# Attention and a two-layer MLP on one core: w_in asked behind the first value chunk, fifteen small matmuls in front, and a held Pool copy moved behind an addition

## The chip, the cores and the metric

The kernel runs on one core of a Trainium2 chip. The core has a matrix engine (PE, whose weight loads the profile lists as PEld), a vector engine (DVE), a scalar engine for activations (ACT), a general engine (Pool, also written POOL or GpSimd), a queue engine (SP), and 16 DMA engines that move data between the off-chip memory, HBM, and the on-chip memory, SBUF. PE writes its results to PSUM, an accumulation memory of eight banks; DVE and ACT read them from there. All engines run their own list of instructions in order and wait for each other through semaphores.

The metric is device time in microseconds (us). Three runs of the kernel before took 312.16, 312.55 and 313.92 us; the median is 312.55.

## The reference, cut to what matters

Inputs q, k and v have 8 batches, 8 heads, 576 positions and 64 features. Each batch gets two attentions whose results are added, and the sum goes through two matrix products with a quick GELU between them.

```python
factor = 4
q_d = q.reshape(B, H, Sd, factor, D).mean(axis=3)       # k_d, v_d likewise: 144 positions
out_up = np.repeat(sm_attn(q_d, k_d, v_d), factor, axis=2)
mask = np.abs(pos[:, None] - pos[None, :]) < factor     # local attention, 7 neighbours
scores = np.where(mask, scale * q @ k.T, -1e9)
out_local = softmax(scores) @ v
x = (out_up + out_local).transpose(0, 2, 1, 3).reshape(4608, 512)
h = x @ w_in                                            # 512 x 2048
g = h * sigmoid(1.702 * h)
out = g @ w_out                                         # 2048 x 512
```

## The kernel before, in words

The order of the work is written out by hand: each engine's instructions stand in the order in which the code calls them, and semaphores are put in where one needs the other's result.

The MLP works on nine groups of 512 tokens. In a group, `mm1` computes 16 chunks of 128 hidden features, each from four matmuls of 128x512 over `xT` (the attention's output, transposed, in four tiles of 128 features) and `w_in_bf` (line 813, called through `hps_mm`); ACT applies the activation (line 824). `mm2` then makes four tiles of 128 tokens from 16 matmuls each with `w_out_bf` (line 891). The attention of the next batch is cut into steps that are called at fixed places between these matmuls: `POS_0` lists the places for group 0, `POS` those for the later groups. Place 16 is the first matmul of `mm2`. For batch 1 the steps are: scores of the first four heads, their exponentials, scores and exponentials of the other four, and then one step for each of the four pairs of heads (`avx1`). The last of a pair's work is an addition (line 664) that adds the coarse attention to the local one in `xT`; for the first three pairs Pool does it, for the fourth DVE. The products in front of it are DVE's (line 653), which reads copies that it took out of PSUM (line 642) and ACT's logarithms and exponentials (lines 637 and 648).

Batch 0 has nothing to hide behind. Its attention runs first, and group 0 starts behind it. At the start, DVE sets constants while Pool asks for batch 0's k and q (line 218) and for its values in five chunks (line 259, `load_vb0`). PE begins with `warm(2)`, two float32 matmuls on zeros (line 777), writes the mask into PSUM with `bars0` (line 411) and then computes scores (line 423) as soon as DVE has transposed q and k (line 311). It reduces the value chunks to the coarse values with selection matrices (line 388, `prep_vd_pe`) in the order of the chunks, and needs chunks 3 and 4 last.

Pool asks for the weights behind batch 0's loads. Two iotas (line 116, `iota_band`) come first, then a copy of one element of value chunk 1 into `gate` (line 943): it holds Pool until that chunk has landed. Then come w_in in three pieces (line 281), batch 1's k and q, and w_out's first two pieces (line 290), then batch 1's values in ten pieces (line 249), w_out's last two pieces and batch 2's k and q. Each of Pool's DMAs uses one of eight semaphores in turn and waits for the landing of the DMA eight before it; so w_out's second piece waits for w_in's first one, and the pieces of batch 1's values for those in between.

Batch 2's float32 values are loaded through SP's queue by `load_v(2, gate=...)` (line 238). Its gate is one more copy of a single element on Pool (line 929), out of w_out's last piece: Pool stands until that has landed, then SP's ten loads may go. In the program before it stands on Pool ahead of batch 1's three additions of line 664. On SP's queue the output stores of group 0 and further loads of batch 2 stand behind the ten loads.

In group 0, `hps_mm` splits the matmuls of the last three of the four feature tiles into two halves of 256 tokens for the first nine chunks, and in group 1 for the first eight; the other matmuls are whole.

Of the kernel before, what the change touches and what calls it, by code (L numbers as in the profile page):

```python
# [19 lines left out]
def kernel(  # L20
# [9 lines left out]
    nc = tc.nc  # L30
# [30 lines left out]
    w_out_bf = persist.tile([128, n_ffc, d_model], BF16, name="w_out_bf")  # L61
    xT = [persist.tile([128, B * S], BF16, name=f"xT{i}") for i in range(HP)]
    vbs = [persist.tile([128, 5, H, 65], BF16, name=f"vb{i}") for i in range(2)]
# [11 lines left out]
    PM = [psum.tile([128, 512], FP32, name=f"pm{i}") for i in range(2)]  # L75
# [3 lines left out]
    def pm_tile():  # L79
        turn["m"] += 1  # L80
        return PM[turn["m"] % 2]

    wz = consts.tile([128, 512], BF16, name="wz")
# [16 lines left out]
    gate = consts.tile([1, 1], BF16, name="gate")  # L100
# [13 lines left out]
    def iota_band():  # L114
        for par in range(2):
            nc.gpsimd.iota(dm[halves[par]], pattern=[[-1, 60]], base=-4 * par,
                           channel_multiplier=1, **it)
# [113 lines left out]
    def load_v(b, gate=None, chunks=range(5)):  # L231
        t = ldp.tile([128, 5, H, D], FP32, name="vf", tag="vf")
        vf[b] = t
        if gate is not None:
            gate(t[0:1, 0, 0, 0:1])
        for i in chunks:
            for par in range(2):
                nc.sync.dma_start(
                    out=t[64 * par : 64 * par + 64, i],
                    in_=bass.AP(  # L240
                        tensor=v.tensor,
                        offset=v[b, 0].offset + (114 * i + KSTART[par]) * D,
                        ap=[[D, 64], [S * D, H], [1, D]],
                    ),
                )
# [12 lines left out]
    def load_vb0(i):  # L258
        nc.gpsimd.dma_start(
            out=vbs[0][:, i, :, 0:D],  # L260
            in_=bass.AP(
                tensor=v.tensor, offset=v[0, 0].offset + 114 * i * D,
                ap=[[D, 128], [S * D, H], [1, D]],
            ),
        )
# [23 lines left out]
    def load_w_out(c):  # L289
        nc.gpsimd.dma_start(  # L290
            out=w_out_bf[:, 4 * c : 4 * c + 4, :],
            in_=bass.AP(
                tensor=moe_w_out.tensor, offset=moe_w_out.offset + c * 512 * d_model,
                ap=[[d_model, 128], [128 * d_model, 4], [1, d_model]],
            ),
        )
# [20 lines left out]
    def prep_qk(b, qd):  # L317
        prep_1("k", b, qd)
        prep_1("q", b, qd)
# [48 lines left out]
    def flat(p):  # L368
        return p.rearrange("p x n -> p (x n)")

    def prep_vd_pe(b, pv, kcs=range(3), eng=None, between=None):
        vb, vd = vbs[b], vds[b]

        def heads(x, j):
            if b == 0:
                return x.rearrange("p (hp j) d -> p hp j d", j=2)[:, :, j]
            return x.rearrange("p (m u j) d -> p m u j d", m=2, u=2)[:, :, j]

        for kc, iis in ((0, (0, 1)), (1, (1, 2, 3)), (2, (3, 4))):
            if kc not in kcs:  # L380
                continue
            c0 = 256 * (kc - kcs[0])
            for i in iis:
                if between:
                    between(kc, i)
                n = S - 114 * i if (b, i) == (0, 4) else 128
                for j in range(2):
                    nc.tensor.matmul(
                        pv[64 * j : 64 * j + 64, c0 : c0 + D * HP],
                        lhsT=psel[b][i // 4][0:n, PSEL_AT[i, kc] : PSEL_AT[i, kc] + 64],  # L390
                        rhs=heads(vb[0:n, i, :, 0:D], j),
                        start=(i == iis[0]), stop=(i == iis[-1]),
                        tile_position=(0, 64 * j),
                    )
        cp = eng.tensor_copy if eng else nc.scalar.copy
        cp(
            out=vd[:, kcs[0] : kcs[-1] + 1, :, 0:D],
            in_=pv[:, 0 : 256 * len(kcs)].rearrange(
                "p (k h d) -> p k h d", k=len(kcs), h=HP
            ),  # L400
        )
# [186 lines left out]
    def sub(t, off, *dims):  # L588
        return bass.AP(
            tensor=t.tensor, offset=t.offset + off,  # L590
            ap=[list(t.ap[0])] + [list(d) for d in dims],
        )
# [181 lines left out]
    def warm(n, t=None):  # L774
        t = pm_tile() if t is None else t
        for _ in range(n):
            nc.tensor.matmul(
                sub(t, 0, (256, 2), (1, 256)), lhsT=wzf[:, 0:128],
                rhs=wzf[:, None, :].to_broadcast([128, 2, 256]),
                start=True, stop=True,  # L780
            )

    def attention(b):
        st = {}

        def s_pe(qd):
            P = PB if b == 1 else PA
            st["d", qd], st["s", qd] = scores_mixed(b, qd, P)

        def s_act(qd):  # L790
            if qd == 0:
                nc.scalar.preload_act_table_set("natural_log_exp_and_others")
            if qd:
                exp_down(qd, st["d", qd])
            exp_local(qd, st["s", qd], (1, 0) if qd else (0, 1))
            if not qd:
                exp_down(qd, st["d", qd])
            mask_local(qd)

        def s1():  # L800
            s_pe(1)
            s_act(1)

        first = [lambda: s_pe(0), lambda: s_act(0), s1]
        if b == 1:
            return first + [lambda hp=hp: avx1(b, hp) for hp in range(HP)]
        return first + [lambda: avx(b, (0, 1)), lambda: avx(b, (2, 3))]

    def hps_mm(g, ffc, dmc, acc):
        halved = dmc and (ffc < 9 if g == 0 else g == 1 and ffc < 8)  # L810
        n = TG // 2 if halved else TG
        for c in range(0, TG, n):
            nc.tensor.matmul(  # L813
                acc[:, c : c + n],
                lhsT=w_in_bf[:, dmc, ffc * 128 : (ffc + 1) * 128],
                rhs=xT[dmc][:, g * TG + c : g * TG + c + n],
                start=(dmc == 0), stop=(dmc == n_dmc - 1 and c + n == TG),
            )

    def new_gT():  # L820
        return moe_sb.tile([128, n_ffc, TG], BF16, name="gT", tag="gT")
# [101 lines left out]
    POS_0 = [16, 18, 28, 40, 48, 58, 69]  # L923
# [4 lines left out]
    def after(src, eng):  # L928
        return lambda t: eng.tensor_copy(out=t, in_=src)
# [9 lines left out]
    fill()  # L939
    for i in range(5):  # L940
        load_vb0(i)
    iota_band()
    nc.gpsimd.tensor_copy(out=gate, in_=vbs[0][0:1, 1, 0, 0:1])
    load_w_in(0, 512)
    load_w_in(512, 512)
    load_w_in(1024, 1024)
    for qd in range(NQ):
        load_qk(1, qd)
    load_w_out(0)
    load_w_out(1)  # L950
    warm(2)
    make_up()
    make_psel0()
# [6 lines left out]
        rhs=wzf[:, None, 0:196].to_broadcast([128, 2, 196]),  # L960
        start=False, stop=True, skip_group_check=True,
# [79 lines left out]
    for g in range(n_groups):  # L1041
        b = g + 1
        if g == 0:
            for i in range(5):
                load_vb(1, i)
            load_w_out(2)
            load_w_out(3)
            for qd in range(NQ):
                prep_qk(1, qd)
                reduce_qk(1, qd, "k")  # L1050
                reduce_qk(1, qd, "q")
                load_qk(2, qd)
            make_psel1()
            nc.gpsimd.memset(v4[32:64], 0.0)
            load_v(2, gate=after(w_out_bf[0:1, 12, 0:1], nc.gpsimd))
        elif b < B:
            load_v4(b)
            prep_qk(b, 0)
            pool_qk(b, 0)
            if 2 < b < B - 1:  # L1060
                for qd in range(NQ):
                    load_qk(b + 1, qd)
            prep_v(b, nc.gpsimd)
            if b + 1 < B:
                load_v(b + 1)
            prep_qk(b, 1)
            if b == 2:
                reduce_qk(b, 1, "k")
                reduce_qk(b, 1, "q")
            else:  # L1070
                pool_qk(b, 1)
            prep_v4(b, nc.gpsimd, (0,))
            if b == 2:
                for qd in range(NQ):
                    load_qk(b + 1, qd)
            prep_v4(b, nc.gpsimd, (1, 2))
        steps = {}
        if b < B:
            for n, f in zip(POS if g else POS_0, attention(b)):
                steps.setdefault(n, []).append(f)  # L1080
            if g == 0:
                steps.setdefault(VDP_0, []).append(lambda: prep_vd_pe(1, flat(PB[2])))
        gT = new_gT() if g else gT0
        mm1(g, gT, steps)
        mm2(g, gT, {n - 16: f for n, f in steps.items() if n >= 16})
# [30 lines left out]
```

## Time and profile before

One execution was profiled.

| what | value |
|---|---|
| time of the profiled execution | 312.91 us |
| its span, first to last instruction | 311.1 us |
| median of three runs | 312.55 us |
| PE busy | 302.7 us, 97% of the span |
| ACT, DVE, Pool busy | 203.3, 149.6, 147.6 us |
| granted PE clock | 1.000 |
| DMA traffic | 39.94 MB in 64042 packets |
| PE instruction blocks fetched | 32, 0.52 MB |

How to read it: rows of the timeline give the start and the time taken in us, then the engine, the line, the operation, output and input tile, the shape, the count of instructions merged, and in square brackets the idle time ahead of it and what ended that. The row of a chain gives its start, its length and what took that time; "issue" is time in which the profile shows no wait. Rows of DMA issues give the engine whose queue asked, the count, the size of one in KB (counted in the written type) and the time from the request to the landing. Matmuls overlap: the end of one is modelled, so groups can overlap by some tenths of a us.

### The profile page before, as it was taken

The page shows a single profiled execution, that of the slowest core. Times are in us where ns is not written, and L with a number is a line of the kernel's source. Part 1 is how long each engine was busy: PE and PEld are TensorE (multiplying, and loading weights), DVE is VectorE, ACT ScalarE, POOL GpSimd, SP SyncE. Part 2 cuts the span into 40 slices and gives each one's busy share as a digit, 9 for nine tenths or more (in the row PEclk, how much of TensorE's full clock was granted, in tenths as well). Part 3 has the DMA queues.
Part 4 walks back from the last instruction along what each step waited for, and adds up shares of the span by engine and source line. Part 5 has one row for each costly group of instructions (what it writes and reads, how often), then busy time and mean ns, then how long its engine had stood idle before and what let it go on. Part 6 is the DMA issues. An engine that isn't in the chain of part 4 may idle for free.

```text
span 311.1 us, 9625 instructions
## 1 busy us (share of the span) xinstructions
PE 302.7 (97%) x4175; PEld 157.1 (51%) x4175; DVE 149.6 (48%) x303; ACT 203.3 (65%) x325; POOL 147.6 (47%) x169
## 2 busy tenths in 40 slices
PE   7799999999999999999999999999999999999995
PEld 3477444664544464455545554555455544444444
DVE  5982957762594159505970499028902760000000
ACT  4748755877858786668866895689558857216611
POOL 8542394288029933795369634983396110000000
PEclk9999999999999999999999999999999999999999
DMA  6999999889937942695169715991520110010011
GB/s 107 135 200 211 184 111 209 184 262 174 202 135 168 207 123 77 171 228 139 70 164 202 177 38 170 190 211 46 155 71 34 39 67 2 34 67 36 0 67 67
DMA packets 64042, 39.94 MB, mean 128 GB/s; under 512 B 44544, under 2 KB 54912, under 8 KB 64000
## 3 DMA queue, kind: packets, MB, share of 16 engines
q0 software_dynamic: 18784, 14.95, 34.4%
q1 hardware_dynamic: 45072, 24.32, 28.0%
q8 instruction: 32, 0.52, 0.7%
q14 instruction: 10, 0.08, 0.1%
q10 hardware_dynamic: 144, 0.07, 0.1%
HBM read 44.83 MB, written 9.44 MB: 174 GB/s over the span
## 4 chain that ended last, share of the span: by engine, by line
PE 83%; DMA 11%; ACT 2%; DVE 2%; POOL 1%; issue 1%; POOLq 0%; DVEq 0%; ACTq 0%
PE pm L891 36%; PE pm L813 22%; PE pa L813 14%; DMA w_out_bf<-in_moe_w_out_dram 6%; PE pa L439 3%; DMA vb<-in_v_dram 2%; DMA w_in_bf<-in_moe_w_in_dram 2%; PE pa L700 2%; PE pa L678 2%; PE pa L466 2%; PE pm L908 1%; DVE xT L653 1%; PE pa L891 1%; ACT l L637 1%; ACT l L648 1%
## 5 line engine op out<-in xcount | busy, mean ns | idle before, releaser
L891 PE MATMUL pm<-w_out_bf,gT 128*128 128x512 bf16 x528 | 119.4, 379 | 0.5 <-DMA w_out_bf<-in_moe_w_out_dram 0.5
L813 PEld LDWEIGHTS <-w_in_bf 128*128 128x128 bf16 x627 | 60.6, 98 | 61.7 <-issue 0.3
L813 PE MATMUL pm<-xT,w_in_bf 128*128 128x512 bf16 (+1 forms) x364 | 88.5, 372 | 0.0
L891 PEld LDWEIGHTS <-gT 128*128 128x128 bf16 x560 | 52.7, 98 | 63.0 <-issue 1.1
L824 ACT ACTIVATE gT<-pm 128x512 bf16<-128x512 f32 x88 | 52.8, 604 | 38.8 <-PE pm L813 38.8
L813 PE MATMUL pa<-xT,w_in_bf 128*128 128x512 bf16 (+1 forms) x263 | 59.1, 347 | 0.0
L511 DVE TENSOR_TENSOR es<-es,mask 128x600 bf16<-128x600 bf16 x28 | 18.0, 683 | 82.4 <-ACT es L477 82.4
L876 ACT ACTIVATE osb<-pm 128x512 f32<-128x512 f32 (+2 forms) x35 | 20.3, 581 | 30.5 <-PE pm L891 28.0
L824 ACT ACTIVATE gT<-pa 128x512 bf16<-128x512 f32 x56 | 31.8, 611 | 6.8 <-PE pa L813 6.8
L770 POOL TENSOR_TENSOR xT<-xT,od 128x576 bf16<-128x576 bf16 x12 | 15.8, 1320 | 41.5 <-DVE xT L754 41.4
L754 DVE TENSOR_TENSOR xT<-n,l 128x285 bf16<-128x285 f32 (+1 forms) x96 | 28.1, 364 | 0.0
L342 POOL TENSOR_TENSOR pq<-kT 128x576 f32<-128x576 bf16 x11 | 12.8, 1161 | 30.4 <-DVE kT L311 26.5
L878 DVE TENSOR_SCALAR osb<-pm 128x128 f32<-128x128 f32 x1 | 0.3, 293 | 53.8 <-ACT osb L876 53.8
L359 POOL TENSOR_TENSOR pq<-v 112x512 f32<-112x512 f32 x18 | 23.7, 1318 | 0.8 <-DMA v<-in_v_dram 0.8
L311 DVE STREAM_TRANSPOSE kT<-kb 128x576 f32<-128x576 f32 x16 | 19.9, 1243 | 6.8 <-DMA kb<-in_k_dram 6.8
L311 DVE STREAM_TRANSPOSE qT<-qb 128x576 f32<-128x576 f32 x16 | 19.8, 1237 | 0.3 <-DMA qb<-in_q_dram 0.2
L503 ACT ACTIVATE ed<-pa 128x864 bf16<-128x864 f32 x16 | 14.3, 894 | 7.9 <-PE pa L466 7.9
L477 ACT ACTIVATE es<-pa 128x600 bf16<-128x600 f32 x28 | 17.2, 670 | 0.1
L749 ACT ACTIVATE l<-l 128x1440 f32<-128x1440 f32 x12 | 16.8, 1404 | 0.4
L744 DVE COPY n<-pa 128x492 f32<-128x492 f32 x24 | 15.0, 665 | 2.3 <-ACT l L743 1.7
L743 ACT ACTIVATE l<-pa 128x492 f32<-128x492 f32 x24 | 12.6, 578 | 4.2 <-PE pa L700 3.6
L439 PE MATMUL pa<-qT,kT 32*64 32x60 bf16 x1120 | 15.3, 195 | 0.0
(133 smaller groups left out, 354.2 us busy)
## 6 DMA issues: line engine op xcount, KB each, us to landing
out_dram<-osb SPq DMA_DIRECT2D x34, 256.0 KB, 2.0
vf<-in_v_dram SPq DMA_DIRECT2D x60, 128.0 KB, 4.9
v<-in_v_dram SPq DMA_DIRECT2D x72, 96.0 KB, 2.8
kb<-in_k_dram POOLq DMA_DIRECT2D x16, 288.0 KB, 5.8
qb<-in_q_dram POOLq DMA_DIRECT2D x16, 288.0 KB, 8.6
w_out_bf<-in_moe_w_out_dram POOLq DMA_DIRECT2D x4, 512.0 KB, 18.4
w_in_bf<-in_moe_w_in_dram POOLq DMA_DIRECT2D x2, 512.0 KB, 7.9
w_in_bf<-in_moe_w_in_dram POOLq DMA_DIRECT2D x1, 1024.0 KB, 13.1
```

The source lines that it names most:

```text
L311: nc.vector.transpose(out=t32.rearrange("p (i c) -> p c i", c=18), in_=store[b, qd].bitcast(FP32).rearrange("p (c d) -> p c d", c=18),)
L359: eng.tensor_tensor(out=t1[0:112], in0=x[:, :, 0:2, :], in1=x[:, :, 2:4, :], op=ALU.add)
L439: nc.tensor.matmul(P[1 + r // 2][64 * par : 64 * par + 64, r % 2, 60 * i : 60 * i + 60], lhsT=kT[b, qd][rows, k0 : k0 + 64, a], rhs=qT[b, ...
L477: nc.scalar.activation(out=es[2 * qd + u][:, :, 0:300], in_=sp[u][:, :, 0:300], func=AF.Exp, scale=inv_sqrt_d,)
L511: nc.vector.tensor_tensor(out=ev, in0=ev, in1=mask, op=ALU.mult)
L749: nc.scalar.activation(out=l, in_=l, func=AF.Exp, scale=-1.0)
L754: nc.vector.tensor_tensor(out=out, in0=sub(n, *part), in1=sub(l, *part), op=ALU.mult)
L770: eng.tensor_tensor(out=xs, in0=xs, in1=sub(od[:, u, :], 0, (1, SD), (0, 4)), op=ALU.add)
L813: nc.tensor.matmul(acc[:, c : c + n], lhsT=w_in_bf[:, dmc, ffc * 128 : (ffc + 1) * 128], rhs=xT[dmc][:, g * TG + c : g * TG + c + n], star ...
L824: nc.scalar.activation(out=gT[:, ffc, :], in_=acc, func=AF.Silu, scale=GELU_SCALE)
L876: eng.activation(out=osb, in_=ap, func=AF.Copy, scale=1.0 / GELU_SCALE)
L891: nc.tensor.matmul(ops[t], lhsT=gT[:, ffc, t * 128 : (t + 1) * 128], rhs=w_out_bf[:, ffc, :], start=(ffc == 0), stop=(ffc == n_ffc - 1),)
```

## The change

There are four edits.

1. The copy that holds w_in reads value chunk 0 instead of chunk 1, and it stands ahead of the two iotas instead of behind them. Pool's order is now: five value chunks, copy, two iotas, w_in.
2. A new function `small` issues 15 matmuls of 32 rows, 64 columns of weights and 60 moving columns on the zero tile, in front of `warm(2)`. They go in turn to four places in two PSUM tiles that nothing has used yet.
3. In group 0 only the first four chunks have halved matmuls, not the first nine: five chunks with three matmuls each become whole, 15 matmuls and 15 weight loads fewer. PE's list has as many instructions as before.
4. `load_v(2)` with its gate copy moves into batch 1's step list, behind the first pair's step. On Pool the copy now stands behind the first addition of line 664 and ahead of the second.

```diff
+    def small(n):
+        for i in range(n):
+            r, c = i % 2, i // 2 % 2
+            rows = slice(32 * r, 32 * r + 32)
+            nc.tensor.matmul(
+                PM[r][64 * c : 64 * c + 64, 0:60],
+                lhsT=wz[rows, 0:64], rhs=wz[rows, 0:60],
+                start=True, stop=True, tile_position=(32 * r, 64 * c),
+            )
...
-        halved = dmc and (ffc < 9 if g == 0 else g == 1 and ffc < 8)
+        halved = dmc and (ffc < 4 if g == 0 else g == 1 and ffc < 8)
...
+    nc.gpsimd.tensor_copy(out=gate, in_=vbs[0][0:1, 0, 0, 0:1])
     iota_band()
-    nc.gpsimd.tensor_copy(out=gate, in_=vbs[0][0:1, 1, 0, 0:1])
     load_w_in(0, 512)
...
+    small(15)
     warm(2)
...
             nc.gpsimd.memset(v4[32:64], 0.0)
-            load_v(2, gate=after(w_out_bf[0:1, 12, 0:1], nc.gpsimd))
...
                 steps.setdefault(VDP_0, []).append(lambda: prep_vd_pe(1, flat(PB[2])))
+                steps[POS_0[3]].append(
+                    lambda: load_v(2, gate=after(w_out_bf[0:1, 12, 0:1], nc.gpsimd))
+                )
```

## The prediction

> **What bounds the kernel now.** I read the busy times first, then the busy times by stage, then the chain that ended last in order of time, then each engine's rows around its links.
>
> ```profile
> span 311.1 us, 9625 instructions
> PE 302.7 (97%) x4175; PEld 157.1 (51%) x4175; DVE 149.6 (48%) x303; ACT 203.3 (65%) x325; POOL 147.6 (47%) x169
> q8 instruction: 32, 0.52, 0.7%
> ```
>
> PE is busy for 302.7 of 311.1 us, so only 8.4 us of PE idle time exist. The table by stage says where it lies; its columns are the stage in us, its length, the busy time (and instructions) of PE, weight loads, DVE, ACT and Pool, and then PE's granted clock, the DMA share and GB/s.
>
> ```profile
> 14.00:15.60 1.60, 1.59 (x31) 1.09 (x28) 1.48 (x3) 1.60 (x3) 1.60 (x4) 1.00 0.68 48
> 15.60:20.60 5.00, 4.57 (x121) 3.58 (x117) 3.93 (x8) 2.28 (x6) 2.83 (x5) 1.00 1.18 194
> 20.60:36.00 15.40, 15.40 (x147) 9.85 (x140) 9.66 (x13) 11.09 (x22) 4.84 (x7) 1.00 1.15 209
> 36.00:44.00 8.00, 7.44 (x240) 4.12 (x218) 6.12 (x15) 5.82 (x8) 5.21 (x8) 1.00 2.29 107
> 44.00:58.00 14.00, 13.67 (x195) 6.87 (x192) 9.08 (x24) 7.56 (x14) 7.76 (x8) 1.00 1.09 196
> 58.00:307.00 249.00, 249.00 (x3366) 126.08 (x3364) 108.58 (x212) 167.23 (x261) 116.23 (x119) 1.00 0.48 121
> ```
>
> From 58 us to 307 us PE never stops: nothing that the change does there can shorten the kernel. Between 20.6 and 58 us PE misses 0.56 us (8.00 - 7.44) and 0.33 us (14.00 - 13.67), together 0.89 us: the ceiling of any gain behind batch 0's attention. The rest lies before 20.6 us, in batch 0's attention, which loads and DVE set. The chain shows what holds the 0.56 us:
>
> ```profile
> 5.42 7.57 DMA vb<-in_v_dram
> ...
> 13.27 7.05 DMA w_in_bf<-in_moe_w_in_dram
> ...
> 20.61 18.57 DMA w_out_bf<-in_moe_w_out_dram
> ...
> 39.23 1.02 PE pm L891 x4
> ```
>
> Value chunk 1 lands at 12.99, the gate copy lets Pool ask for w_in at 13.27, w_in's first piece lets Pool ask for w_out's second piece at 20.61, and PE, whose work in front of it ends 0.48 us too soon, waits until that lands at 39.18.
>
> **The change, part by part.** First the gate. Pool's rows, and the issue-to-landing rows of the value chunks 1 and 4 of batch 0 (issued at 5.42 and 8.02) and of batch 1's last value piece:
>
> ```profile
> 4.48 4.45 POOL L259 DMA_DIRECT2D vb<-in_v_dram  x5
> 8.90 0.48 POOL L116 IOTA dm<- 64x60 f32 x2
> 13.04 0.18 POOL L943 COPY gate<-vb 1x1 bf16<-1x1 bf16 x1 [3.66 <-DMA vb<-in_v_dram]
> 39.47 2.03 POOL L249 DMA_DIRECT2D vb<-in_v_dram  x3 [2.52 <-DMA w_out_bf<-in_moe_w_out_dram]
> 51.54 0.43 POOL L929 CAST vf<-w_out_bf 1x1 f32<-1x1 bf16 x1 [3.71 <-DMA w_out_bf<-in_moe_w_out_dram]
> 51.94 1.20 POOL L664 TENSOR_TENSOR xT<-xT,od 128x576 bf16<-128x576 bf16 x1
> 53.68 1.21 POOL L664 TENSOR_TENSOR xT<-xT,od 128x576 bf16<-128x576 bf16 x1 [0.54 <-DVE xT L653]
> ```
>
> ```profile
> vb<-in_v_dram POOLq DMA_DIRECT2D x1, 128.0 KB, 7.8
> vb<-in_v_dram POOLq DMA_DIRECT2D x1, 64.0 KB, 3.4
> ```
>
> Chunk 1 landed at 12.99, chunk 4 at 8.02 + 7.8 = 15.82: three chunks in 2.83 us, 0.94 each, so chunk 0 landed near 12.05 (estimated from these rows). The new gate copy runs at 12.10, ends at 12.28; the two iotas that now stand behind it take 0.48; w_in is asked at about 12.82 instead of 13.27, 0.45 us earlier. The table has the room for it: between 14.0 and 15.6 us the DMA moves 48 GB/s, after that 194, a hole of 1.6 x (1 - 48/194) = 1.2 us. From 15.6 to 36 us the stream is full, so an earlier start should move all behind it by the same 0.45: batch 1's k and q, w_out and batch 1's values. Bounds: 0 (the value chunks' tail holds w_in back as now) to 1.2 us (the hole vanishes). I take 0.45, which comes from the events themselves. The iotas' consumer, the mask, is made by DVE only behind batch 0's normalisation; moving them costs nothing more.
>
> What that is worth on PE:
>
> ```profile
> 36.40 0.51 PE L439 MATMUL pa<-qT,kT 32*64 32x60 bf16 x40
> 39.23 1.02 PE L891 MATMUL pm<-w_out_bf,gT 128*128 128x512 bf16 x4 [0.48 <-DMA w_out_bf<-in_moe_w_out_dram]
> 44.32 0.30 PE L388 MATMUL pa<-vb,psel 128*64 128x256 bf16 x2 [0.18 <-DVE es L511]
> 53.29 1.24 PE L891 MATMUL pm<-w_out_bf,gT 128*128 128x512 bf16 x5
> 54.68 0.25 PE L603 MATMUL pa<-ed,vd 48*64 48x144 bf16 x2
> ```
>
> w_out's second piece lands at 38.73 instead of 39.18; PE restarts at 38.78 and gains 0.45 of the 0.48. At 44.32 PE waits 0.18. The row names DVE, but the two products read batch 1's last value chunk, whose last piece, issued third in the group at 39.47, so at about 40.8, landed 3.4 later, at 44.2. That stream moves 0.45 forward as PE does: the 0.18 stays. Sum of the first part: -0.45 (0 to -0.66).
>
> Second, Pool's held copy. Before, it waits at 51.54 for w_out's last piece, and behind it stand batch 1's three additions. DVE at that time:
>
> ```profile
> 48.38 0.96 DVE L653 TENSOR_TENSOR xT<-n,l 128x285 bf16<-128x285 f32 x4
> 49.45 0.99 DVE L642 COPY n<-pa 128x300 f32<-128x300 f32 x2
> 51.48 2.12 DVE L653 TENSOR_TENSOR xT<-n,l 128x285 bf16<-128x285 f32 x4
> 53.70 0.99 DVE L642 COPY n<-pa 128x300 f32<-128x300 f32 x2
> ```
>
> The four products at 51.48 take 2.12 us, those at 48.38 only 0.96: the difference, 1.16, is the length of Pool's addition at 51.94 (1.20), which ran beside them. The addition's operand was ready at 49.34. Moved ahead of the copy it runs from about 49.4 to 50.6, beside DVE's copies out of PSUM, which do not suffer: 0.99 at 53.70 beside Pool's addition at 53.68, 0.99 at 49.45 without one. So DVE gains up to 1.16 us, the copy at 53.70 comes earlier, so does ACT's logarithm that waits for it, and PE, which had finished at 54.53 (53.29 + 1.24) and restarted at 54.68, loses its 0.15 us of waiting. More is not there, since PE has no other hole up to 307 us. The copy itself still waits for the same landing (now 0.45 earlier), so the ten value loads of batch 2 on SP's queue, and the output stores and batch 2's further loads behind them, go out no later; the second addition, now behind the copy, is ready after it. If the copy's 0.43 us fell on DVE's products instead, 0.7 of the 1.16 would still remain. Part two: -0.15 (0 to -0.15).
>
> Third, 15 small products (with 15 weight loads) ahead of the warm-up, and five chunks of batch 0 whose three later products are no longer halved: 15 products and weight loads fewer there.
>
> ```profile
> 4.77 0.41 PE L411 MATMUL pa<-off,id 128*128 128x120 bf16 x2
> 8.35 0.23 PE L423 MATMUL pa<-qT,kT 32*128 32x120 bf16 x2 [1.35 <-DVE qT L311]
> 23.08 1.47 PE L813 MATMUL pa<-xT,w_in_bf 128*128 128x256 bf16 x12
> 29.62 6.25 PE L813 MATMUL pm<-xT,w_in_bf 128*128 128x512 bf16 x28
> ```
>
> The nearest shape is the 32-row, 60-column product: 40 in 0.51, 0.013 each, 0.2 us for 15; the upper bound from two 120-column products in 0.41 right after the start is 0.2 each, 3.1 us. They delay the warm-up and the bars behind it. PE then idles 1.35 us until DVE's q transpose, so 0.2 costs nothing, the upper bound would cost 1.7. I take 0.2, by shape, so 0 on the path. Halves cost 2 x 1.47/12 = 0.24, wholes 6.25/28 = 0.22: a gain of 15 x 0.02 = 0.3 at most, but the groups' ends are modelled, and the shorter group carries its tail over fewer products. Twice 256 columns are 512 columns; I take 0.
>
> The sum is -0.45 - 0.15 = -0.60 on the profiled execution, 312.91 to 312.31. That execution lies 0.36 above the median of the three runs, 312.55; on the median: 311.95. Half a per cent, 1.56 us, is about what a measurement of this kernel can tell from no change.
>
> **Rivals.**
>
> *An instruction block meets the last value chunks (slower).* The 15 pairs shift what PE fetches. The page has 32 blocks for 8350 PE instructions, one per 261. This is one block's traffic, in 13.9 to 16 us:
>
> ```profile
> q8 instruction: 1, 0.02, 4.1%
> ```
>
> 4.1% of 16 engines over 2.1 us is 1.38 us on one DMA engine. Thirty instructions earlier it would be asked for ahead of 14 us, while value chunks 3 and 4 still move. PE's two products on chunk 4 follow its landing at once:
>
> ```profile
> 15.86 0.30 PE L388 MATMUL pm<-vb,psel 120*64 120x256 bf16 x2
> ```
>
> A landing later by x delays batch 0's attention, and with it PE's unbroken run from 20.6 us on, by x. All that can absorb it are the waits of 0.48, 0.18 and 0.15, together 0.81: it decides above x = 0.81, and at x = 1.38 the sum is +0.57, 313.1. For it: the landing at 15.82 has no slack. Against: the chunk's rows are spread over 16 engines and mostly moved by 14.0 (48 GB/s from there). The Trainium skill, "Runtime: NRT & Kernel Launch", section "Instruction fetch mechanics", calls the cost of crossing a 16 KiB block mostly hidden; by that rule x is 0 and 311.95 stands. PE's unbroken stage to 307 us agrees, while no run here shows a block inside these chunks. The skill's "DMA: Bandwidth & Descriptors", section on queues, rings and completion order, says that an engine turns between its queues packet by packet, which would let a whole block stand in front, x up to 1.38.
>
> *The earlier request gains nothing.* The stream is bound by the value chunks and full from 15.6 us, and w_out lands at 39.18 as before. Then only 0.15 is left: 312.4. For it: w_out's second piece shares its stage with batch 1's value pieces (36 to 44 us, DMA share 2.29), which could set its landing; against: the hole of 1.2 us.
>
> *More than counted.* The hole closes and the 0.18 at 44.32 goes too, and chunk 4 lands earlier: -0.66 - 0.15 - 0.2 = -1.0, 311.5.
>
> **How the numbers follow.** Forecast 0.45, no gain from the request 0.14, more 0.11, the block (or small products above the 1.35 us) 0.30. The block alone ends within half a per cent even at its full price; beyond +1.56 it comes only with the small products' upper bound on top (1.38 + 1.7), a third of this case: 0.10, and 0.01 for what is unseen make slower by over 0.5% 0.11. Faster by over 0.5% needs 1.56 where 0.89 is the ceiling behind 20.6 us, so the rest from batch 0's attention: 0.07. The remaining 0.82 is within. The range takes the "more" case and a low run, 311.1, and the block case at its full price with as much above it, 313.5. The forecast's own range is 311.5 to 312.4.
>
> **What the changed profile would show.** The gate copy near 12.1 and w_in asked near 12.8; w_out's second piece landing near 38.7 and no wait above 0.1 us at PE's ninth product of the second layer; Pool's first addition near 49 us and the second head's four products back at about 1 us; PE's wait before the third head's products gone; the score products of batch 0 still starting at 8.35. Wrong if batch 0's chunk 4 lands after 16.4, if the first scores slip beyond 8.5, or if w_out's second piece lands at 39.2 again.

## The result, and the profile after

The changed kernel takes 311.79 us (median of 22 runs, 311.41 to 312.23), the kernel before 312.58 us on the same chips (22 runs, 311.98 to 314.39). The ratio is 0.9971 with a 95% interval of 0.9961 to 0.998. The change is a gain of 0.8 us, 0.3%: certain, because so many runs stand behind it, and inside the half per cent that the prediction had called no change. The forecast was 311.95. Between the two profiled executions the gain is 1.2 us: the time went from 312.91 to 311.70, the span from 311.1 to 309.9. 0.3 of that is the profile of before lying above its median.

The head of the page of the changed kernel:

```profile
span 309.9 us, 9625 instructions
PE 303.5 (98%) x4175; PEld 156.4 (50%) x4175; DVE 148.1 (48%) x303; ACT 203.6 (66%) x325; POOL 147.8 (48%) x169
q8 instruction: 32, 0.52, 0.7%
```

PE's idle time fell from 8.4 to 6.4 us, a part of it only because the small products fill the start; the counts of instructions and of instruction blocks are the same. The table by stage of the changed kernel (stage, length, busy times and counts of PE, weight loads, DVE, ACT and Pool, PE's granted clock, DMA share, GB/s) says where:

```profile
14.00:15.60 1.60, 1.59 (x30) 1.07 (x27) 1.48 (x3) 1.60 (x3) 1.60 (x3) 1.00 1.26 148
15.60:20.60 5.00, 4.62 (x123) 3.55 (x119) 3.99 (x9) 2.35 (x6) 2.65 (x5) 1.00 1.23 208
20.60:36.00 15.40, 15.40 (x129) 8.42 (x125) 11.27 (x15) 11.09 (x22) 4.77 (x7) 1.00 1.18 206
36.00:44.00 8.00, 7.93 (x233) 4.50 (x214) 4.75 (x14) 6.15 (x9) 6.11 (x10) 1.00 1.71 118
44.00:58.00 14.00, 14.00 (x197) 7.28 (x196) 9.11 (x29) 9.59 (x16) 6.02 (x5) 1.00 1.04 197
58.00:306.00 248.00, 248.00 (x3359) 125.45 (x3357) 106.72 (x207) 165.03 (x259) 116.73 (x118) 1.00 0.48 120
```

The hole of the load stream between 14.0 and 15.6 us has filled from 48 to 148 GB/s, and PE's missing time from 36 to 58 us has shrunk from 0.56 + 0.33 to 0.07 us. From there to 306 us PE is busy without a break, as it was before. PE's rows of the changed kernel, to be held against the five of the prediction:

```profile
36.33 0.51 PE L439 MATMUL pa<-qT,kT 32*64 32x60 bf16 x40
36.78 2.76 PE L901 MATMUL pm<-w_out_bf,gT 128*128 128x512 bf16 x12
42.58 0.97 PE L388 MATMUL pa<-vb,psel 128*64 128x256 bf16 x14
52.21 1.24 PE L901 MATMUL pm<-w_out_bf,gT 128*128 128x512 bf16 x5
```

Line 901 is line 891 of before. The first twelve products of the second layer are now one row, and so are the fourteen selection products: the waits of 0.48 and 0.18 us, which stood inside these rows and cut them, have gone. The score products start 0.07 us earlier than before (36.40), the five products of line 901 by 1.08 us (53.29): 1.0 us of the gain arises between these two rows. The rest comes at the wait behind them; the three products of the second layer that follow there start at 54.17 instead of 55.48, 1.31 us earlier, of which 1.2 are left at the end. The gain is larger than the waits that the rows show (0.48 + 0.18 up to there, 0.15 behind it, 0.81 in all), because the end of a matmul is modelled: products of 512 columns start 0.216 us apart in this trace and are drawn 0.38 long, so a row hides about 0.16 us of a wait behind its last product. From start to start the three waits were worth 0.64, 0.37 and 0.24.

Pool's rows of the changed kernel show why the waits went (line 952 is the copy into `gate`, line 939 the held copy):

```profile
4.49 4.46 POOL L259 DMA_DIRECT2D vb<-in_v_dram  x5
11.86 0.18 POOL L952 COPY gate<-vb 1x1 bf16<-1x1 bf16 x1 [2.91 <-DMA vb<-in_v_dram]
11.99 0.41 POOL L116 IOTA dm<- 64x60 f32 x2
12.35 2.27 POOL L281 DMA_DIRECT2D w_in_bf<-in_moe_w_in_dram  x3
18.60 0.75 POOL L290 DMA_DIRECT2D w_out_bf<-in_moe_w_out_dram  x1 [1.10 <-DMA w_in_bf<-in_moe_w_in_dram]
48.42 1.21 POOL L664 TENSOR_TENSOR xT<-xT,od 128x576 bf16<-128x576 bf16 x1 [2.20 <-DVE xT L653]
49.88 0.17 POOL L939 CAST vf<-w_out_bf 1x1 f32<-1x1 bf16 x1 [0.25 <-DMA w_out_bf<-in_moe_w_out_dram]
51.45 1.21 POOL L664 TENSOR_TENSOR xT<-xT,od 128x576 bf16<-128x576 bf16 x1 [1.40 <-DVE xT L653]
```

w_in is asked at 12.35 instead of 13.27, 0.92 us earlier; its first piece lets Pool ask for w_out's second piece at 18.60 instead of 20.61, 2.0 us earlier. That piece landed at 37.53 (before 39.18), and the last piece of batch 1's values at 43.10 (before 44.19); both now come before PE needs them.

The 2.0 us are more than the 0.92 of the request. A load ends in 16 parts in this trace. Of w_in's first piece, 15 had landed at 18.80 before and the sixteenth at 20.32, 1.52 us later; now they end at 18.13 and 18.32. What differs beside the request is the first of the 32 PE instruction blocks in the trace, which moved from 14.53 to 13.93 us and took 1.4 us in both. The experiments come back to it.

DVE's rows of the changed kernel:

```profile
47.31 0.96 DVE L653 TENSOR_TENSOR xT<-n,l 128x285 bf16<-128x285 f32 x4
50.41 0.96 DVE L653 TENSOR_TENSOR xT<-n,l 128x285 bf16<-128x285 f32 x4
51.47 1.00 DVE L642 COPY n<-pa 128x300 f32<-128x300 f32 x2
```

Pool's addition at 48.42 runs ahead of the products at 50.41, which are back at 0.96 us from 2.12. The second addition, at 51.45, lies beside the copies out of PSUM at 51.47, which take 1.00 as they do alone.

The start, PE's first rows in the changed kernel:

```profile
1.19 0.43 PE L787 MATMUL pm<-wz 32*64 32x60 bf16 x15 [1.19 <-DVE wz L126]
1.55 3.78 PE L777 MATMUL pm<-wz 128*128 128x512 f32 x4
8.37 0.23 PE L423 MATMUL pa<-qT,kT 32*128 32x120 bf16 x2 [0.20 <-DVE qT L311]
```

The fifteen small products delay the warm-up by 0.36 us, and the scores start at 8.37 (before 8.35), behind an idle time of 0.20 instead of 1.35.

### The profile page after: what moved, and what is told of

Its sections match the earlier page's. It is cut to its first block, busy times and chain, and to the rows that moved or that the text cites. A ratio compares the mean times of both kernels' runs of the same rounds, so it can differ in the third digit from the quotient of the medians.

```text
span 309.9 us, 9625 instructions
## 1 busy us (share of the span) xinstructions
PE 303.5 (98%) x4175; PEld 156.4 (50%) x4175; DVE 148.1 (48%) x303; ACT 203.6 (66%) x325; POOL 147.8 (48%) x169
## 4 chain that ended last, share of the span: by engine, by line
PE 94%; DVE 2%; DMA 2%; ACT 1%; issue 0%; POOL 0%; DVEq 0%; ACTq 0%; POOLq 0%
PE pm L901 37%; PE pm L823 25%; PE pa L823 16%; PE pa L439 3%; PE pa L901 2%; PE pa L700 2%; PE pa L678 2%; PE pa L466 2%; DMA qb<-in_q_dram 2%; PE pm L918 1%; DVE qT L311 1%; PE pa L575 1%; PE pa L615 1%; PE pa L603 0%; PE pm L388 0%; PE pa L520 0%
## 5 line engine op out<-in xcount | busy, mean ns | idle before, releaser
L823 PEld LDWEIGHTS <-w_in_bf 128*128 128x128 bf16 x612 | 59.2, 98 | 63.1 <-issue 0.3
```

The source lines that it names most:

```text
L823: nc.tensor.matmul(acc[:, c : c + n], lhsT=w_in_bf[:, dmc, ffc * 128 : (ffc + 1) * 128], rhs=xT[dmc][:, g * TG + c : g * TG + c + n], star ...
```

## The experiments

Each edit alone, each pair of edits, and then variants of the two edits that turned out to matter. Kernels that were measured on one chip in turn share their runs of the kernel before, so equal numbers in the third column are the same runs. "w_in" is the time at which Pool asks for it, "block" the start of the first PE instruction block in the trace, "last part" how long the sixteenth part of w_in's first piece landed behind the fifteenth, "w_out" the landing of its second piece; these four are read from the one profiled execution of each kernel.

| kernel | median, us | before, us | ratio (95% interval) | w_in | block | last part | w_out |
|---|---|---|---|---|---|---|---|
| before | | 312.58 | | 13.27 | 14.53 | 1.52 | 39.18 |
| changed | 311.79 | 312.58 | 0.9971 (0.9961 to 0.998) | 12.35 | 13.93 | 0.19 | 37.53 |
| gate_only | 312.46 | 312.61 | 1.0003 (0.9987 to 1.002) | 12.15 | 15.54 | 1.33 | 38.43 |
| small_only | 312.56 | 312.61 | 1.0004 (0.9994 to 1.0014) | 12.80 | 14.33 | 0.31 | 38.13 |
| move_only | 312.72 | 312.61 | 1.001 (0.9993 to 1.0027) | 12.79 | 15.01 | 1.70 | 39.30 |
| no_move | 311.76 | 312.61 | 0.998 (0.9971 to 0.9988) | 12.12 | 13.91 | 0.11 | 37.81 |
| no_gate_edit | 312.77 | 312.63 | 0.9994 (0.9979 to 1.0009) | 13.12 | 14.49 | 0.17 | 38.48 |
| no_small | 312.72 | 312.63 | 1.0003 (0.9983 to 1.0023) | 12.07 | 17.10 | 0.01 | 37.51 |
| small_27 | 311.87 | 312.63 | 0.9978 (0.9966 to 0.999) | 12.25 | 14.08 | 0.81 | 37.27 |
| unheld | 312.22 | 312.63 | 0.9988 (0.9975 to 1.0002) | 9.34 | 16.06 | 0.96 | 37.20 |
| long_warm | 311.72 | 312.44 | 0.9971 (0.9954 to 0.9988) | 12.35 | 14.59 | 1.21 | 37.82 |
| late_gate | 313.90 | 312.44 | 1.0043 (1.0027 to 1.0059) | 14.15 | 14.18 | 0.08 | 39.37 |
| small_15_halves | 313.57 | 312.44 | 1.0037 (1.0019 to 1.0054) | 11.89 | 14.04 | 1.11 | 37.23 |
| small_2 | 311.86 | 312.80 | 0.9975 (0.9961 to 0.9988) | 12.16 | 14.48 | 0.86 | 37.69 |

**Each edit alone.** gate_only is the kernel before with edit 1, small_only with edits 2 and 3, move_only with edit 4.

```diff
# gate_only, against before
-    iota_band()
-    nc.gpsimd.tensor_copy(out=gate, in_=vbs[0][0:1, 1, 0, 0:1])
+    nc.gpsimd.tensor_copy(out=gate, in_=vbs[0][0:1, 0, 0, 0:1])
+    iota_band()
```

> The first edit alone: w_in behind chunk 0 and two iotas. My theory (the earlier request moves the whole stream): w_in asked near 12.4 instead of 13.27, w_out's second piece landing at 38.3 or before, the waits at 39.23 and 44.32 gone, 0.7 to 0.9 us off the span, ratio about 0.9975; the products of the second head still take 2.1 us. Rival (the instruction block, not the request, set w_in's first landing): the block stays near 14.5, w_in's first piece still lands 6 to 7 us behind its request with w_out's second piece at 38.9 to 39.2, at most 0.3 us gained.

```diff
# small_only, against before
-        halved = dmc and (ffc < 9 if g == 0 else g == 1 and ffc < 8)
+        halved = dmc and (ffc < 4 if g == 0 else g == 1 and ffc < 8)
...
+    small(15)
     warm(2)
```

> The 15 small products and the 15 halves less, alone. My theory: nothing on the path, span within 0.1 us of before, the wait at 39.23 still 0.4 to 0.5. Rival (the block's place matters): the block comes near 13.9, w_in's first piece lands near 18.8 instead of 20.3 though it is asked at 13.27, w_out's second piece lands near 38.5 and 0.4 to 0.7 us are gained.

```diff
# move_only, against before
             nc.gpsimd.memset(v4[32:64], 0.0)
-            load_v(2, gate=after(w_out_bf[0:1, 12, 0:1], nc.gpsimd))
...
+                steps[POS_0[3]].append(
+                    lambda: load_v(2, gate=after(w_out_bf[0:1, 12, 0:1], nc.gpsimd))
+                )
```

> Pool's held copy behind the first addition, alone. My theory: the second head's four products take 0.96 instead of 2.12, the wait before the third head (0.15) goes, 0.15 to 0.3 us off the span, waits at 39.23 and 44.32 unchanged. Rival (the addition collides with DVE's copies instead): the copies at 49.4 grow beyond 1.2 us and nothing is gained.

None of the three differs from before: the gains that were expected of gate_only and move_only did not come, and small_only's time is the one expected, though in its profile the wait for w_out is gone. In gate_only w_in is asked 1.1 us earlier, and the wait for w_out goes; but the block comes at 15.54, in the middle of w_in's first piece, w_out's second piece is only 0.75 us earlier, and batch 1's last value piece becomes the wait. In move_only Pool's first addition lies where the prediction wanted it, and the two waits that the load stream sets stay. PE's waiting rows behind 20 us, first of gate_only, then of move_only:

```profile
43.99 0.30 PE L388 MATMUL pa<-vb,psel 128*64 128x256 bf16 x2 [0.59 <-DMA vb<-in_v_dram]
```

```profile
39.35 1.02 PE L901 MATMUL pm<-w_out_bf,gT 128*128 128x512 bf16 x4 [0.43 <-DMA w_out_bf<-in_moe_w_out_dram]
44.49 0.30 PE L388 MATMUL pa<-vb,psel 128*64 128x256 bf16 x2 [0.24 <-DVE es L511]
```

The profiled execution of small_only (311.83 us) is the fastest of its twelve. It waits for no load there, but its products on batch 1's values take 1.35 us, where the changed kernel's row has 0.97: PE stands for 0.13 us ahead of the third of them (at 42.78, with "issue" as releaser). The median, 0.7 us above, suggests that most of its executions lose more; no profile shows where.

```profile
42.35 1.35 PE L388 MATMUL pa<-vb,psel 128*64 128x256 bf16 x14
```

**Each edit left out.** no_move has all but edit 4, no_gate_edit all but edit 1, no_small all but edits 2 and 3; each is the changed kernel with the diff above taken back.

> The changed kernel with the held copy back in its old place: gate and small products only. My theory: 0.15 to 0.3 us slower than the changed kernel, 0.8 to 1.0 us faster than before, with the second head's products back at 2.1 us. Rival (the gains do not add, the copy's move is hidden once the stream is early): same span as the changed kernel within 0.1 us.

> The changed kernel with the gate edit undone: small products and the moved copy only, w_in asked near 13. Theory after the first runs (both the early request and the block's new place are needed, since either one alone leaves w_out's second piece or batch 1's last value piece landing at the edge of PE's need): the block near 14, w_in's first piece without a straggler, but about 312.3 to 312.6, as the small products alone gave. Rival (the small products and the move carry the gain, the single run of the products was unlucky): 311.8 to 312.0.

> The changed kernel without the small products, with the nine halved chunks back: gate and moved copy only. Theory (both needed): the block at 14.5 to 15.6 inside w_in's first piece, whose last part lands 1.3 us or more behind the others, batch 1's last value piece at 43.8 or later, 312.2 to 312.5. Rival (the gate and the move together do it, the products are idle): 311.7 to 311.9.

no_move is as fast as the changed kernel: the moved copy is worth nothing beside the other two. Pool's and DVE's rows of no_move show what became of the clash:

```profile
49.70 0.17 POOL L939 CAST vf<-w_out_bf 1x1 f32<-1x1 bf16 x1 [3.26 <-DMA w_out_bf<-in_moe_w_out_dram]
49.85 1.20 POOL L664 TENSOR_TENSOR xT<-xT,od 128x576 bf16<-128x576 bf16 x1
```

```profile
50.28 0.94 DVE L653 TENSOR_TENSOR od<-n,l 128x144 f32<-128x144 f32 x1 [0.81 <-ACT l L648]
51.15 0.95 DVE L653 TENSOR_TENSOR xT<-n,l 128x285 bf16<-128x285 f32 x4
```

With the stream early, w_out's last piece lands before 49.7, so the addition starts 1.5 us behind the products at 47.41 that it needs (they end at 48.37), not 2.6 as before (49.34 to 51.94). The addition still slows a product of DVE, the one at 50.28 (0.94 instead of 0.31), but no PE wait follows.

no_gate_edit keeps a PE wait for the values, and its time is that of before. So edit 1 is needed.

```profile
44.67 0.30 PE L388 MATMUL pa<-vb,psel 128*64 128x256 bf16 x2 [1.11 <-DMA vb<-in_v_dram]
```

no_small has the earliest request of the three and w_out's piece at 37.51, and its time is that of before all the same. PE's rows of no_small:

```profile
18.56 0.27 PE L575 MATMUL pa<-id,y 128*128 128x117 bf16 x2
19.56 0.21 PE L575 MATMUL pa<-id,y 128*128 128x114 bf16 x1 [0.73 <-issue]
```

PE stands for 0.73 us inside a run of ready products, with no engine or load that it waits for. The first instruction block began at 17.10 there, 3 us later than in the changed kernel and later than the 14.5 to 15.6 that were expected. Its twelve executions run from 311.53 to 315.0 us, so the loss is not in every one. So the small products, which the prediction took for harmless, are needed as well; the question is for what.

**What the small products are for.** Four variants of the changed kernel, all with edits 1 and 4. In small_27 all halves of group 0 are gone and 27 small products lead: PE's list has the same length. In long_warm and small_2 the nine halved chunks of before are kept; a third float32 warm-up, or two small products, make PE's list longer by two products. small_15_halves keeps the nine halved chunks behind 15 small products, so that it is longer by 15.

```diff
# small_27, against the changed kernel
-        halved = dmc and (ffc < 4 if g == 0 else g == 1 and ffc < 8)
+        halved = dmc and g == 1 and ffc < 8
...
-    small(15)
+    small(27)
```

> The changed kernel with 27 small products and no halved chunk in group 0, so the block moves another 24 instructions forward at the same number of instructions. If it only has to be out of w_in's first piece: block near 13.4 to 13.8, chunk 4 still landing near 15.8, the same time as the changed kernel, 311.6 to 312.0. If a block inside the value chunks delays them (the slower rival of the prediction): chunk 4 lands after 16.2 and the time is 0.4 to 1.2 us above the changed kernel. First scores still near 8.4; if 27 products (0.8 us by the 15 that took 0.36) reach past DVE's transpose they start near 8.6.

```diff
# long_warm, against the changed kernel
-        halved = dmc and (ffc < 4 if g == 0 else g == 1 and ffc < 8)
+        halved = dmc and (ffc < 9 if g == 0 else g == 1 and ffc < 8)
...
-    small(15)
-    warm(2)
+    warm(3)
```

> The changed kernel without the small products and with nine halved chunks, but with a third float32 warm-up product: PE is busy longer at the start by 1.7 us at most, with one instruction more, not thirty. Theory (the number of instructions counts, since it sets when the first block is asked for): the block stays behind w_in's request, at 15 to 17, PE runs dry for some tenths between 18 and 20 or w_in's first piece has a straggler above 0.4 us, 312.2 to 312.9. Rival (the extra early work on PE counts): block near 13.9 or no such wait, 311.6 to 311.9.

```diff
# small_2, against the changed kernel (halves as in long_warm)
-    small(15)
+    small(2)
     warm(2)
```

> The gate edit and the move with nine halved chunks, and two small products ahead of two warm-ups: PE's list is longer by two instructions, as with the third warm-up that gave 311.72, but PE's start is no longer busy. If the place of the instructions decides: about 311.7, first scores at 8.4 behind an idle time of about 1.4, the first instruction block before 15, no 0.7 us hole around 18 to 20 us. If the busy start (or the later first scores) decides: 312.5 to 312.9, as without any small product, the block behind 16 us and PE dry by about 0.7 us near 19.6.

```diff
# small_15_halves, against the changed kernel
-        halved = dmc and (ffc < 4 if g == 0 else g == 1 and ffc < 8)
+        halved = dmc and (ffc < 9 if g == 0 else g == 1 and ffc < 8)
```

> The changed kernel with nine halved chunks, so PE has 30 instructions more than before and every later block comes 30 instructions earlier. If only the first block matters: 311.6 to 312.0, the same as the changed kernel. Rival (the fewer halves keep later blocks in good places): a new wait without a releaser on PE behind 60 us and 312.2 or more.

long_warm was meant to tell whether the count of early instructions matters; it came out as fast as the changed kernel (311.72), and the theory that the fifteen are needed fell with it. But it is longer than no_small by two products and two weight loads, so it left open whether its busy start or these four entries of PE's list did it. small_2 tells: it has the same four entries and an idle time of 0.67 us ahead of the scores, and it takes 311.86 where no_small takes 312.72. The two ran on different chips and their intervals just overlap (0.9961 to 0.9988, 0.9983 to 1.0023); the difference of the ratios, 0.28%, is clear of zero all the same (about 0.1 to 0.5%, an estimate from all their runs), and long_warm and small_27 stand on small_2's side. Four entries are enough; 15 or 27 products bring nothing more. The same stretch of PE's rows in small_2, without a stop:

```profile
18.47 0.32 PE L575 MATMUL pa<-id,y 128*128 128x117 bf16 x3
18.63 0.27 PE L575 MATMUL pa<-up,y 128*128 128x167 bf16 x2
```

small_15_halves shows the same thing further down. With 30 entries more in front of batch 1's scores, its PE rows are

```profile
40.02 0.26 PE L439 MATMUL pa<-qT,kT 32*64 32x60 bf16 x7
41.72 0.18 PE L439 MATMUL pa<-qT,kT 32*64 32x60 bf16 x1 [1.44 <-issue]
```

a stop of 1.44 us with no releaser, and not behind 60 us, where a wait had been expected. To see what these stops have in common, PE's records, products and weight loads together, were counted from the start of the trace. The table gives, for each stop, the entry at which PE stopped, the instruction block that landed last before it went on, and the time between the two (unheld and late_gate follow further down).

| kernel | stop, us | entry | block began, ended | PE went on | behind the block's end |
|---|---|---|---|---|---|
| no_small | 0.73 | 448 | 17.10, 18.10 | 19.56 | 1.46 |
| unheld | 0.73 | 448 | 16.06, 17.04 | 18.26 | 1.22 |
| small_15_halves | 1.44 | 1213 | 38.86, 40.42 | 41.72 | 1.30 |
| late_gate | 0.52 | 1211 | 40.85, 42.60 | 44.29 | 1.69 |
| small_only | 0.13 | 1215 | 39.32, 40.93 | 42.78 | 1.85 |

The traces of small_15_halves and late_gate lack some records of products: late_gate's holds 8307 products and weight loads, where the complete ones of the same length hold 8350. (A missing record shows as a gap of 0.16 us with "issue" ahead of a 512-column product, in these two and in long_warm; that is no stop.) late_gate stops at the same product as small_only, the third on batch 1's values, and small_only's trace is complete; so the entries 1211, 1213 and 1215 are one place, near 1216. Five stops, in four different lines of the code, thus stand at two places of the list. The first place follows the first block of the trace, the second follows the fourth: three blocks for about 768 entries, 256 each.

Each stop ends 1.2 to 1.9 us behind the end of a block. The reading is that PE stops because the next block isn't there. The trace names no releaser, but in none of the fourteen traces does PE pass either place less than 1.2 us behind the end of its block. The delay is not a fixed one: gate_only passes the first place without a stop 1.39 us behind its block (18.74 and 17.35), move_only 1.45. The changed kernel has more room, 2.15 us at the first place (17.46 and 15.31) and 1.97 at the second (42.61 and 40.64), and so has small_2 at the first, 2.5.

In small_15_halves the second place falls among the dense score products and is reached at 40.28, before its block has ended; in the changed kernel it falls 2.3 us later, behind eight products of the second layer. small_15_halves takes 1.8 us more than the changed kernel (313.57 - 311.79), and the stop is 1.44 of that. A second cost lies behind its last product: its trace shows a 33rd block, begun at 313.11 where the span has ended at 311.3, and in five of its twelve executions the time exceeds the span by 1.9 to 2.7 us, in all runs of the other variants by 1.7 to 1.9. Against this edit 3 helps: it takes back the entries that edit 2 puts in front.

Why the block at 14 us is late in some kernels can be seen from the 260th entry, about the last one that no prompt block precedes: in the kernels where the block is prompt, it begins 0.05 to 1.2 us behind that entry. The entry is a yardstick for this stretch alone, since the third block of each trace begins 3.7 to 5.1 us ahead of the entry 512 further on. The time from w_in's request to the 260th entry is 0.77 us in the kernel before, 0.98 in the changed one, 1.69 in long_warm and 1.70 in small_2, all prompt; 1.78 in gate_only, where the block begins 1.6 us behind the entry; 2.03 in no_small and 3.9 in unheld, where it begins 3.0 and 2.8 us behind it. So the order of the two requests separates the kernels: a block that is asked for more than about 1.7 us after w_in comes late, as if it stood among w_in's rows. Edit 1 moves w_in ahead; without small products the 260th entry is the first selection product on batch 0's values (line 388), which starts at 14.10 in no_small; with two small products that entry lies ahead of these (13.86), with fifteen among the scores (13.33). That fits gate_only, where edit 1 brings the block late and gains nothing. With edits 2 and 3 and the late request the block is prompt (14.33 in small_only, 14.49 in no_gate_edit), and what is left is the late stream: no_gate_edit's wait of 1.11 us for the values. The limit of 1.7 us is read from one profiled execution of each kernel.

**When to ask for w_in.** unheld is the changed kernel without the copy that holds w_in. late_gate holds it for value chunk 2 with the iotas behind the copy, and has edit 4 and the nine halved chunks, no small products.

```diff
# unheld, against the changed kernel
-    nc.gpsimd.tensor_copy(out=gate, in_=vbs[0][0:1, 0, 0, 0:1])
     iota_band()
...
# late_gate, against the changed kernel without edits 2 and 3
-    nc.gpsimd.tensor_copy(out=gate, in_=vbs[0][0:1, 0, 0, 0:1])
+    nc.gpsimd.tensor_copy(out=gate, in_=vbs[0][0:1, 2, 0, 0:1])
```

> The changed kernel without the copy that holds w_in: w_in is asked right behind the two iotas near 9.4. If the requests are served in order: value chunks land as before (chunk 4 near 15.8), w_out's second piece earlier by up to 1 us, but no wait of PE is left to remove, so 311.6 to 312.0. If w_in's rows mix with the value chunks': chunk 4 lands 0.5 us or more later, batch 0's attention slips by as much, 312.3 to 313.5.

> Gate on value chunk 2 with the two iotas behind it, no small products, nine halved chunks: w_in asked near 14.4, about when PE asks for its first block. Theory (what counts for the block is whether it goes ahead of w_in's rows): the block at 14.4 to 14.8, w_in's first piece with a straggler below 0.5 us, PE never dry, but w_out's second piece not before 39 and batch 1's last value piece behind 44: 312.5 to 313.2. Rival (the block is late by itself): block behind 15 again.

Asking at 9.34 instead of 12.35 doesn't bring w_in's first piece earlier (18.50 against 18.32), probably because of the value chunks in front, the last of which landed at 15.59. The block, though, came at 16.06, and PE stood for 0.73 us at 18.26, so the 311.6 to 312.0 that were expected became 312.22:

```profile
18.26 0.21 PE L533 MATMUL pa<-vd,ed 48*128 48x65 bf16 x2 [0.73 <-issue]
```

late_gate has no small products, so its nearest neighbour is no_small, with chunk 0 in place of chunk 2: 313.90 against 312.72. Its first block is prompt (14.18) and the last part only 0.08 late, but w_in is asked 2.1 us later; w_out's second piece landed at 39.37, and PE waited for it, for the values and, by the reading above, for a block, where a PE that never runs dry had been expected:

```profile
39.41 1.02 PE L901 MATMUL pm<-w_out_bf,gT 128*128 128x512 bf16 x4 [0.69 <-DMA w_out_bf<-in_moe_w_out_dram]
44.29 0.53 PE L388 MATMUL pa<-vb,psel 128*64 128x256 bf16 x6 [0.52 <-issue]
45.30 0.41 PE L388 MATMUL pa<-vb,psel 128*64 128x256 bf16 x4 [0.48 <-DMA vb<-in_v_dram]
```

Of the places tried, chunk 0 gives the lowest time: without a holding copy the block comes late, behind chunk 2 the loads do. unheld is not clearly slower, though, as its interval (0.9975 to 1.0002) overlaps that of the changed kernel.

## Why the prediction was right, step by step

*The bound.* Right: PE's three waits between 38 and 55 us were all that could be gained behind batch 0's attention, and PE is unbroken from there on. The ceiling of 0.89 us was too low, since each of the shown waits hides 0.09 to 0.19 us of its length; from start to start it was 1.2 us.

*The gate.* The mechanism was right and its size too small. The term was 0.45 us and the request moved by 0.92 (by 0.83 in the mean of the profiles: 11.89 to 12.35 in the eight kernels where chunk 0 holds it, 12.79 to 13.27 in the four with chunk 1): chunk 0 landed at 11.80, not at 12.05, because the chunks do not land at even distances, and the copy and the iotas took 0.49 from 11.86 on where 0.72 had been counted. For w_out's second piece the forecast was 38.73, the landing 37.53: a part of that goes with the sixteenth part of w_in's first piece, which the prediction had no term for.

*The wait of 0.18 us was to stay.* Wrong. The prediction moved batch 1's values by the same 0.45 as PE; they moved by 1.09 and PE at that place by 0.7. This is the "more than counted" rival, of which the mechanism (both waits gone) came true, while chunk 4 of batch 0 landed as before (15.77 against 15.82). It had a chance of 0.11 and a time of 311.5; the median lies between it and the forecast.

*The held copy.* Right in each row (addition at 48.42, products back at 0.96, PE's wait gone) and wrong in its worth: no_move reaches the same time without it. The term of 0.15 was counted beside the gate's, and the earlier landing of w_out's last piece had taken it already.

*The small products.* They took 0.43 us where 0.2 had been counted, and nothing of it lies on the path: right, as far as their own time goes. The step that failed is that the edit was costed by the time of its matmuls alone. It left out that every entry of PE's list moves the places at which a block has to be there. no_small and small_2 show that two small products are worth 0.86 us beside the earlier request, and small_15_halves that, behind 15 small products, the halves taken back are worth 1.8. So that the forecast came so close is in part luck, since two errors met: too little for the gate with the others' help, and nothing for the others. The gate by itself, which the sum gave 0.45 us, gained nothing (gate_only, no_small).

*The instruction block.* The slower rival had the right object and the wrong victim. The block did move 0.6 us forward and took 1.38 us, exactly the price worked out, but chunk 4 was not delayed. The Trainium skill, "Runtime: NRT & Kernel Launch", section "Instruction fetch mechanics", calls the cost of such a block mostly hidden; that holds for the changed kernel and not for no_small, unheld, small_15_halves and late_gate, where PE stood for 0.73, 0.73, 1.44 and 0.52 us. In those the measurement decides.

*The rival that the request gains nothing* fell with the 18.60 and the 37.53.

What stays open: whether a block and the loads hold each other up on one DMA engine, which the records do not name, and how the longest executions of gate_only and no_small (314.32 and 315.0) look, since one execution of each was profiled. That the edits belong together, and that edits 2 and 3 shift the two places, is shown by times and rows; that PE stands there for want of a block rests on the five stops and the ends of their blocks; that w_in's rows are what delays the block rests on the order of requests alone.

## What to carry to other kernels

An edit that adds or removes instructions on a full engine moves every later place at which that engine needs its next block of instructions, and this can be worth more than the instructions: here 1.8 us for 15 small products too many, 0.86 us for two in the right place. So read, beside the durations, when the blocks land, and look for stops with "issue" as their releaser at the same entry of the engine's list. When several edits share one load stream, test the pairs as well as each alone: here no edit alone gains anything, two together gain all, and the third is worth nothing beside them.

## What the runs showed that was not expected

PE can stand still in the middle of ready work, by all signs because it has run out of instructions: 0.73 us twice, 0.13, 0.52 and 1.44, at the same two places of its list, and it goes on 1.2 to 1.9 us behind the end of the block that it lacks.

One block of 16 KB takes 0.9 to 2.5 us (0.995 in no_small, 2.519 in move_only). In the kernels where it began between 14.48 and 15.54 us, with w_in under way, the sixteenth part of w_in's first piece came 0.86 to 1.70 us behind the fifteenth, except in no_gate_edit (block at 14.49, 0.17). Where it began by 14.33, or at 17.10 (no_small), it was 0.01 to 0.31, except in small_27 (0.81) and small_15_halves (1.11); unheld had 0.96 with the block at 16.06. So the block may be one cause of the late part, and is not the only one.

A wait of PE that the trace shows is too short, as the end of the product before it is modelled: three waits of 0.48, 0.18 and 0.15 us in the rows were 0.64, 0.37 and 0.24 from start to start.
